# One output store for two batches: the shared 64-row blocks stored by a single transfer over 128 partitions

## Chip, cores and metric

The kernel runs on one core of one Trainium2 chip. The metric is device time in microseconds (us) of one execution. Where a profile is read, it is one profiled execution, and its span leaves out a little that the timed figure includes (435.0 us of span against 436.74 us for that same execution of the kernel before).

## The reference, cut to what matters

A causal attention with forget gates over 8 batches, 8 heads and 576 positions gives `x` of shape (8, 576, 512). A spectral mix over the sequence, with 64 modes, gives `y`, and the output is formed from both:

```python
u = x + y
return (u + np.maximum(u @ w_ch, 0.0)).astype(np.float32)   # (8, 576, 512)
```

Only the last stage matters here: the output, 9.44 MB in float32, is written to DRAM.

## The kernel before

A batch has 576 rows: four blocks of 128 and one of 64. To fill all 128 partitions, the 64-row blocks of two batches share one block: batch `b` lies on partitions 0 to 63, batch `b + 1` on 64 to 127. The last stage handles, for each of four pairs of batches, four "full" jobs (256 rows each) and then one shared block:

```python
jobs = []
for bp in range(B // 2):
    jobs += [(b, sb, 2) for b in (2 * bp, 2 * bp + 1) for sb in (0, 2)]
    jobs.append((2 * bp, 4, 1))          # the shared block
...
def emit_u(job, ps, split=False):
    uo = wpool.tile([128, 2, 2, D], F32, tag="wb", name="uo")   # ring of 9 buffers
    ...                                                         # ACT: uo[:, 0] <- PSUM

def emit_o(job, ps, uo, split=False):
    ...
        nc.vector.scalar_tensor_tensor(          # relu(u @ w_ch) + u
            uo[:, 1, bs, :], ps[1][:, bs, :], 0.0, uo[:, 0, bs, :],
            ALU.max, ALU.add,
        )
        if sb == 4:                              # shared block: two stores of 128 KB
            for h in range(2):
                eng = (nc.sync, nc.scalar)[h]
                eng.dma_start(
                    out[b + h, 512:576, :],
                    uo[64 * h : 64 * h + 64, 1, 0, :],
                )
        else:                                    # full job: 512 KB on SP
            nc.sync.dma_start(
                out[b, 128 * sb : 128 * sb + 256, :].rearrange(
                    "(p r) e -> p r e", r=2
                )[:, bs, :],
                uo[:, 1, bs, :],
            )
```

`nc.sync` issues on SP, `nc.scalar` on ACT. The first full job is stored in two halves, so there are 17 full-job stores, of which 5 come before the first shared block and 12 after it.

The softmax here doesn't subtract the row's maximum and nothing guards it: scores larger than these inputs give would overflow.

## Time and profile before

| | before |
|---|---|
| time, median of 3 runs | 439.09 us (435.85 to 439.66) |
| profiled span | 435.0 us |
| first output store issued | 404.62 us |
| last output store issued, landed | 430.33 us, 433.49 us |

The last three come from the trace's instruction records. The profile page of the kernel before shows the packets of all DMA traffic and of the hardware queues (q1 is SP's, q10 is ACT's; the columns are packets, MB, and the time that the packets took as a share of 16 engines' span):

```profile
span 435.0 us, 12214 instructions
...
DMA packets 50693, 97.37 MB, mean 224 GB/s; under 512 B 3760, under 2 KB 12944, under 8 KB 50640
...
q1 hardware_dynamic: 3632, 9.91, 6.3%
...
q10 hardware_dynamic: 320, 0.52, 0.3%
```

Packets under 512 B are completion packets of 4 bytes, apart from a few: on the hardware queues a transfer ends with one on each DMA engine that took part. The ACT queue carries only the four second halves of shared blocks: 320 packets = 4 x (64 rows + 16 completions). So each of those stores ran on 16 engines. This reading is used throughout: completion packets on a hardware queue count the engines.

The windows view of the kernel before, over the store stage (the last two columns are the mean busy share of the 16 DMA engines and the rate):

```profile
core 0: us, PE busy (x) PEld busy (x) DVE busy (x) ACT busy (x) POOL busy (x), PEclk, DMA share, GB/s
...
410.00:415.00 5.00, 4.90 (x63) 2.70 (x57) 3.69 (x5) 3.54 (x4) 0.26 (x1) 1.00 0.99 361
415.00:420.00 5.00, 4.55 (x59) 2.45 (x53) 4.11 (x4) 3.03 (x5) 0.00 (x0) 1.00 0.98 364
420.00:425.00 5.00, 4.40 (x52) 2.73 (x54) 4.02 (x5) 3.43 (x5) 0.00 (x0) 1.00 0.99 394
425.00:430.00 5.00, 3.50 (x40) 1.62 (x35) 4.33 (x5) 2.70 (x4) 0.00 (x0) 1.00 0.94 354
430.00:435.00 5.00, 0.00 (x0) 0.00 (x0) 0.29 (x1) 0.00 (x0) 0.00 (x0) 0.73 0.53 184
```

From 410 us on the DMA engines have next to no free time, 0.94 to 0.99, while PE, DVE and ACT each have some.

The view of the two store lines in the kernel before, L988 for shared blocks and L993 for full jobs (issue time on the queue in ns as least/median/most, and time from issue to landing):

```profile
L988 SPq DMA_DIRECT2D out_dram<-uo x4: 472/484/529, 410.1 to 430.3; - x4
L988 ACTq DMA_DIRECT2D out_dram<-uo x4: 501/504/570, 410.1 to 430.3; - x4
...
DMA to landing us min/median/max: 2.9/3.9/5.2
```

```profile
L993 SPq DMA_DIRECT2D out_dram<-uo x17: 332/333/367, 404.6 to 429.7; - x17
...
DMA to landing us min/median/max: 2.1/3.8/5.2
```

And what SP waited for in the kernel before (total us, times, longest); L1081 is the end of the program:

```profile
SPq L993 <- DVE uo L981: 20.0, 16, 4.0
...
SPq L1081 <- DMA out_dram<-uo: 2.6, 2, 1.7
```

### The profile page before, as it was taken

The numbers are of one execution on the slowest core, as the hardware profiler recorded it, in microseconds if no ns is written. First come the engines' busy times: TensorE is split into PE (matmuls) and PEld (weight loads), VectorE is DVE, ScalarE is ACT, GpSimd is POOL, SyncE is SP. The second block draws the span as 40 slices with busy tenths as digits, with TensorE's granted clock in tenths as the row PEclk, the third lists the DMA queues.
The fourth block names the chain that finished last, engine by engine and source line by source line (L and its number), as shares of the span: only waits on it lengthen the run. The fifth ranks groups of instructions, "written<-read, shape, count | busy, mean of one in ns | idle before, by whom it ended". The sixth has DMA issues, their size and how long they took to land.

```text
span 435.0 us, 12214 instructions
## 1 busy us (share of the span) xinstructions
PE 359.7 (83%) x5247; PEld 246.9 (57%) x5265; DVE 263.3 (61%) x658; ACT 225.3 (52%) x340; POOL 128.8 (30%) x202
## 2 busy tenths in 40 slices
PE   2687799999987877778878797899999987798984
PEld 1454566776665665565656565666665544554552
DVE  5677778877465655646657577523324544644875
ACT  3689378775626356364374554143344433633763
POOL 7333332153233233232333222232322232200600
PEclk9998689998868668577587779599999989989998
DMA  8999999999999999999999999999999999995697
GB/s 182 234 236 240 235 236 239 235 204 238 233 216 237 220 228 237 211 237 228 217 237 211 211 211 212 211 211 211 211 212 211 211 211 211 211 211 115 231 380 282
DMA packets 50693, 97.37 MB, mean 224 GB/s; under 512 B 3760, under 2 KB 12944, under 8 KB 50640
## 3 DMA queue, kind: packets, MB, share of 16 engines
q0 software_dynamic: 46688, 86.16, 101.2%
q1 hardware_dynamic: 3632, 9.91, 6.3%
q8 instruction: 41, 0.67, 0.6%
q10 hardware_dynamic: 320, 0.52, 0.3%
q14 instruction: 12, 0.10, 0.1%
HBM read 163.73 MB, written 9.44 MB: 398 GB/s over the span
## 4 chain that ended last, share of the span: by engine, by line
PE 35%; DMA 27%; ACT 12%; DVE 10%; issue 4%; DVEq 0%; POOL 0%; ACTq 0%
DMA wb<-in_moe_w_i_dram 26%; ACT E L559 8%; PE pav L597 7%; PE A L186 6%; PE ps L552 6%; PE tp L500 5%; PE px L640 3%; PE pz L806 2%; DVE QTs L515 2%; ACT KT L513 2%; PE vp L524 2%; DVE uo L981 2%; DVE XT L654 1%; DVE E L574 1%; PE pu L806 1%
## 5 line engine op out<-in xcount | busy, mean ns | idle before, releaser
L559 ACT ACTIVATE E<-ps 128x1024 bf16<-128x1024 f32 (+1 forms) x128 | 101.5, 854 | 24.1 <-PE ps L552 14.8
L186 PE MATMUL A<-XT,wb 128*128 128x16 bf16 x1984 | 70.1, 181 | 12.8 <-DMA wb<-in_moe_w_i_dram 7.8
L91 POOL DMA_DIRECT2D wb<-in_moe_w_r_dram x64 | 42.5, 663 | 126.6 <-PE A L186 30.2
L186 PEld LDWEIGHTS <-wb 128*128 128x128 bf16 x1984 | 63.4, 99 | 26.8 <-issue 11.6
L552 PE MATMUL ps<-QTs,KT 64*128 64x64 bf16 (+4 forms) x384 | 56.0, 315 | 18.1 <-ACT E L559 16.7
L91 POOL DMA_DIRECT2D wb<-in_moe_w_i_dram x64 | 42.4, 663 | 80.5 <-DMA wb<-in_moe_w_i_dram 38.1
L597 PE MATMUL pav<-va,E 128*128 128x65 bf16 (+1 forms) x1088 | 53.5, 206 | 4.2 <-DVE x_all L619 3.7
L597 PEld LDWEIGHTS <-E 128*128 128x128 bf16 (+1 forms) x1088 | 44.0, 112 | 20.1 <-issue 9.5
L574 DVE TENSOR_TENSOR E<-E,trimask 128x256 bf16<-128x256 bf16 (+2 forms) x128 | 37.3, 303 | 20.0 <-ACT E L559 19.7
L517 ACT COPY VT<-tp 128x640 bf16<-128x640 bf16 (+1 forms) x32 | 23.2, 755 | 33.2 <-PE tp L500 33.0
L845 ACT CAST XW<-pxw 128x512 bf16<-128x512 f32 x36 | 20.7, 587 | 35.7 <-PE pxw L838 30.8
L888 ACT CAST XW<-pB 128x512 bf16<-128x512 f32 x36 | 21.0, 586 | 31.8 <-PE pB L806 25.3
L552 PEld LDWEIGHTS <-KT 64*128 64x128 bf16 x384 | 19.0, 97 | 30.3 <-issue 21.3
L887 DVE CAST x_all<-pA 128x512 bf16<-128x512 f32 x36 | 24.9, 692 | 16.6 <-PE pA L806 15.7
L838 PE MATMUL pxw<-wch,yy 128*128 128x512 bf16 x133 | 33.7, 385 | 1.1 <-issue 0.5
L513 ACT COPY KT<-tp 128x640 bf16<-128x640 bf16 (+1 forms) x32 | 22.1, 754 | 22.2 <-PE tp L500 22.2
L515 DVE COPY QTs<-tp 128x640 bf16<-128x640 bf16 (+1 forms) x32 | 23.2, 768 | 14.2 <-PE tp L500 14.0
L619 DVE TENSOR_TENSOR x_all<-pav,rcp 128x384 bf16<-128x384 f32 x64 | 29.1, 455 | 0.8
L608 DVE RECIPROCAL rcp<-pav 128x6 f32<-128x6 f32 x64 | 12.1, 190 | 22.8 <-PE pav L597 22.1
L151 DVE TENSOR_TENSOR YTe<-A,Yacc 128x128 bf16<-128x128 f32 x16 | 5.9, 367 | 33.1 <-PE A L186 33.1
L806 PEld LDWEIGHTS <-ident_bf 64*64 64x64 bf16 (+1 forms) x300 | 15.9, 109 | 15.8 <-issue 8.2
L981 DVE SCALAR_TENSOR_TENSOR uo<-pz,uo 128x1024 f32<-128x1024 f32 (+1 forms) x21 | 21.9, 1070 | 4.6 <-PE pu L806 1.5
(141 smaller groups left out, 636.1 us busy)
## 6 DMA issues: line engine op xcount, KB each, us to landing
wb<-in_moe_w_r_dram POOLq DMA_DIRECT2D x62, 512.0 KB, 17.1
wb<-in_moe_w_i_dram POOLq DMA_DIRECT2D x62, 512.0 KB, 17.6
out_dram<-uo SPq DMA_DIRECT2D x15, 512.0 KB, 3.8
stv<-in_v_dram POOLq DMA_DIRECT2D x10, 576.0 KB, 15.4
stk<-in_k_dram POOLq DMA_DIRECT2D x11, 288.0 KB, 15.5
stq<-in_q_dram POOLq DMA_DIRECT2D x11, 288.0 KB, 15.3
wx<-in_v_dram POOLq DMA_DIRECT2D x5, 576.0 KB, 15.1
wx<-in_k_dram POOLq DMA_DIRECT2D x5, 288.0 KB, 15.7
```

The lines of the kernel that those rows point to most:

```text
L91: tc.keep_in_program_order(nc.gpsimd.dma_start(dst, src))
L186: nc.tensor.matmul(A[:, eb, mi, :], lhsT=w_of(mi, eb * 128), rhs=x_of(m), start=(i == 0), stop=(i == len(terms) - 1),)
L513: nc.scalar.copy(rows(KTs[pr % 2][:, :, 0:S]), tv)
L515: nc.vector.tensor_copy(rows(QT[pr][:, :, :]), tv)
L552: nc.tensor.matmul(ps[:, b, o : o + n], lhsT=KTs[pr % 2][bs, h, jb * 128 : (jb + 1) * 128], rhs=QT[pr][bs, h, jb * 128 + c0 : jb * 128 + c ...
L559: nc.scalar.activation(E[:, :, piece * 512 : piece * 512 + w], ps[:, :, 0:w], ACT.Exp, scale=scale,)
L574: nc.vector.tensor_tensor(dg, dg, tr, ALU.mult)
L597: nc.tensor.matmul(pav[64 * half : 64 * half + w, slot, :], lhsT=E[:, b, c : c + (w - 1) * st + 1 : st], rhs=va[:, jb, b, :], start=(n == ...
L619: nc.vector.tensor_tensor(xo, pi, ri, ALU.mult)
L806: return nc.tensor.matmul(p, lhsT=lhsT, rhs=rhs, start=first, stop=not first, skip_group_check=True)
L838: nc.tensor.matmul(pxw[:, :], lhsT=xT[:, eb, i * 128 : (i + 1) * 128], rhs=wch[:, eb, :], start=(eb == 0), stop=(eb == NDC - 1),)
L981: nc.vector.scalar_tensor_tensor(uo[:, 1, bs, :], ps[1][:, bs, :], 0.0, uo[:, 0, bs, :], ALU.max, ALU.add,)
```

## The change

The intent is to save one of two issues per shared block and to free ACT from storing. The destination is written as two batches x 64 rows x 512, the source is all 128 partitions:

```diff
                 if sb == 4:
-                    for h in range(2):
-                        eng = (nc.sync, nc.scalar)[h]
-                        eng.dma_start(
-                            out[b + h, 512:576, :],
-                            uo[64 * h : 64 * h + 64, 1, 0, :],
-                        )
+                    dst = out[b, 512:576, :]
+                    nc.sync.dma_start(
+                        bass.AP(
+                            tensor=dst.tensor,
+                            offset=dst.offset,
+                            ap=[[S * D, 2], [D, S - 512], [1, D]],
+                        ),
+                        uo[:, 1, 0, :],
+                    )
```

Bytes, addresses and the 2 KB contiguous runs are the same. The order of work on PE, DVE and POOL is unchanged.

## The prediction

> **What bounds the kernel now.** The change touches only the store stage, the last 30 us of a 435.0 us span (page). By the windows view the DMA engines are 0.98 to 0.99 busy at 361 to 394 GB/s from 410 to 425 us, all of it output stores. In the trace's packets a 4096-byte packet takes 163 ns and a 2048-byte one 84 to 94 ns, so each of the 16 engines gives about 25 GB/s: the stage is near its DMA limit. The last two stores are issued at 430.3 us and land at 433.5 us; 1.5 us of closing follow.
>
> **What the change does.** Four times, two 64-partition stores of 128 KB (SP 0.48 us, ACT 0.50 us of issue) become one 256 KB SP store. ACT loses four issues, 2 us in all; it is busy about 65% of this stage and its copies wait for PE, so that is worth tenths of a us. SP's issue count and the order on PE, DVE and POOL stay. Bytes and the 2 KB runs stay.
>
> **The hidden cost: how many engines share a store.** The old destination is 64 rows; the new one is 2 x 64 x 512, slowest dimension 2, beside 128 source partitions. The Trainium skill, "DMA: Bandwidth & Descriptors", section "Why a DMA increments its semaphore by 16 and not by 1", says a DMA uses the largest number of engines up to 16 that divides the slowest non-unit dimension of both sides. For the old stores that gives 16, and the trace agrees: sixteen 4-byte completion packets per store (320 packets on the ACT queue = 4 x (64 + 16)). For the new store it gives 2; no run here shows that yet.
>
> Then two engines move 64 packets of 2 KB each: 64 x 84 ns = 5.4 us per block instead of 0.7 us for both halves. They also carry their 8 packets (1.3 us) of every full store, queued behind. Per batch pair they need 4 x 1.3 + 5.4 = 10.6 us, while a pair now takes 6.76 us (418.62 to 425.38). So they fall behind from the first such store at 410 us: 14 full stores x 1.3 + 4 x 5.4 = 39.8 us, plus about 2 us of start and landing, puts the last landing near 450 to 452 us instead of 433.5. All of it is on the critical path, as only the end follows. Output buffers come round nine jobs later, so compute stalls little.
>
> **Prediction.** +17 us on 439 us (range +9 to +22): 456 us, 448 to 461. Chances: faster 0.01, same 0.12, slower 0.87.
>
> **What would show each step.** Packets under 512 B fall from 3760 to 3640 (128 completion packets removed, 8 added); with 16 engines kept, 3696. The ACT hardware queue (320 packets) vanishes; SP's has 3832. Issue to landing of the block stores grows from 3.9 us to about 7, 11, 15 and 19 us; the full stores behind them grow to some 7, 11, 14 us. After about 434 us no compute engine is busy and the windows show DMA near 0.12 (2 of 16), 50 GB/s, for 15 us. The chain ends with a long DMA out_dram<-uo piece.
>
> **What would make it wrong.** If the transfer is reshaped onto 16 engines, the time stays within 1 us. If engines run faster when only two are active, the loss shrinks toward 10 us; if waiting buffers or a full descriptor queue make SP issue the last block store late, it grows past 20 us.

## The result, and the profile after

| | before | after |
|---|---|---|
| time, median of 4 runs | 438.51 us (435.85 to 439.66) | 453.12 us (452.42 to 454.02) |
| ratio to before | | 1.0343 (1.0291 to 1.0395) |
| profiled span | 435.0 us | 451.3 us |
| first to last output store issued | 404.62 to 430.33 us | 404.58 to 434.52 us |
| from the first store's issue to the end of the span ("the store stage" below) | 30.4 us | 46.7 us |

A ratio here is the mean time of one kernel's fast runs over the mean of the other's fast runs of the same rounds, with a 95% interval, so it is not quite the ratio of the medians. (The kernel before had a fourth run in these rounds, so its median differs from that of the first table.) The first store is issued at the same time in both profiles; all 16.3 us of the longer span come after it.

The page of the kernel after:

```profile
span 451.3 us, 12194 instructions
...
DMA packets 50574, 97.37 MB, mean 216 GB/s; under 512 B 3641, under 2 KB 12825, under 8 KB 50521
...
q1 hardware_dynamic: 3832, 10.44, 6.7%
```

The ACT queue is gone. On SP the packets are 3632 + 200 = 3832: 4 x 64 data packets that ACT had, less 4 x 16 completions of the old SP halves, plus 4 x 2 completions of the new stores. Those 2 are the finding: **each merged store ran on two engines.** (Under 512 B there are 3641; one of them lies on an instruction queue, q14, that has 13 packets in this span and 12 before, and is not the stores'.)

The windows of the kernel after, over the store stage and beyond:

```profile
core 0: us, PE busy (x) PEld busy (x) DVE busy (x) ACT busy (x) POOL busy (x), PEclk, DMA share, GB/s
...
410.00:415.00 5.00, 4.90 (x63) 2.67 (x54) 3.67 (x4) 3.61 (x4) 0.23 (x1) 1.00 0.84 279
415.00:420.00 5.00, 4.54 (x59) 2.41 (x52) 4.11 (x4) 3.03 (x5) 0.00 (x0) 1.00 0.93 334
420.00:425.00 5.00, 4.39 (x52) 2.57 (x54) 4.00 (x5) 3.44 (x5) 0.00 (x0) 1.00 0.58 193
425.00:430.00 5.00, 3.42 (x40) 1.60 (x35) 2.75 (x3) 1.60 (x3) 0.00 (x0) 1.00 0.79 279
430.00:435.00 5.00, 0.00 (x0) 0.00 (x0) 1.82 (x2) 1.11 (x2) 0.00 (x0) 0.69 0.70 254
435.00:440.00 5.00, 0.00 (x0) 0.00 (x0) 0.00 (x0) 0.00 (x0) 0.00 (x0) 0.50 0.66 218
440.00:445.00 5.00, 0.00 (x0) 0.00 (x0) 0.00 (x0) 0.00 (x0) 0.00 (x0) 0.50 0.13 50
445.00:450.00 5.00, 0.00 (x0) 0.00 (x0) 0.00 (x0) 0.00 (x0) 0.00 (x0) 0.50 0.11 45
```

Before 435 us the engines' share already has holes (0.58 at 420 to 425), though the two engines with the merged stores are full. From 440 us no compute engine works and the share is 0.13 and 0.11, about 2 of 16, at 50 and 45 GB/s: two engines empty their queues. In the packets, the merged blocks run from 412.3 us (the first 2048-byte one) to 449.8 us (the last one), at 84 ns each when undisturbed; the late 4096-byte packets take 159 ns. In these 37.5 us each of the two engines has 12 x 8 packets of 4096 bytes and 4 x 64 of 2048 to move, 12 x 1.27 + 4 x 5.4 = 36.8 us of work: they hardly rest.

The store lines of the kernel after are L987 (shared blocks) and L996 (full jobs):

```profile
L987 SPq DMA_DIRECT2D out_dram<-uo x4: 522/598/1153, 410.0 to 434.5; - x4
```

```profile
L996 SPq DMA_DIRECT2D out_dram<-uo x17: 332/807/4821, 404.6 to 433.1; - x17
...
DMA to landing us min/median/max: 2.1/8.1/14.3
```

The full stores land after a median of 8.1 us in place of 3.8, up to 14.3 us, as far as the view can tell (it has the landing of 9 of the 17). Their issue on SP, at most 0.37 us before, takes up to 4.8 us. The view gives no landing for L987, since it expects 16 completions.

What SP waited for in the kernel after (L1084 is the end of the program):

```profile
SPq L996 <- DVE uo L981: 16.7, 14, 3.0
SPq L1084 <- DMA out_dram<-uo: 14.7, 6, 5.6
```

The final wait for stores grew from 2.6 to 14.7 us.

### The profile page after: what moved, and what is told of

It reads as the page before. It is cut to its first block, busy times and chain, and to the rows that moved or that the text cites. A ratio compares the mean times of both kernels' runs of the same rounds, so it can differ in the third digit from the quotient of the medians.

```text
span 451.3 us, 12194 instructions
## 1 busy us (share of the span) xinstructions
PE 365.6 (81%) x5247; PEld 251.2 (56%) x5265; DVE 263.4 (58%) x658; ACT 225.3 (50%) x340; POOL 128.9 (29%) x202
## 2 busy tenths in 40 slices
DMA packets 50574, 97.37 MB, mean 216 GB/s; under 512 B 3641, under 2 KB 12825, under 8 KB 50521
## 3 DMA queue, kind: packets, MB, share of 16 engines
q1 hardware_dynamic: 3832, 10.44, 6.7%
## 4 chain that ended last, share of the span: by engine, by line
PE 33%; DMA 27%; ACT 12%; DVE 9%; issue 4%; DVEq 0%; SPq 0%; POOL 0%; ACTq 0%
DMA wb<-in_moe_w_i_dram 25%; ACT E L559 8%; PE pav L597 7%; PE ps L552 6%; PE A L186 6%; PE tp L500 5%; DMA out_dram<-uo 3%; PE px L640 2%; PE vp L524 2%; ACT KT L513 2%; DVE QTs L515 2%; ACT VT L517 1%; DVE XT L654 1%; PE pz L806 1%; DVE E L574 1%
## 5 line engine op out<-in xcount | busy, mean ns | idle before, releaser
L186 PE MATMUL A<-XT,wb 128*128 128x16 bf16 x1984 | 70.2, 182 | 11.5 <-DMA wb<-in_moe_w_i_dram 6.7
L186 PEld LDWEIGHTS <-wb 128*128 128x128 bf16 x1984 | 63.6, 99 | 25.5 <-issue 11.9
L552 PE MATMUL ps<-QTs,KT 64*128 64x64 bf16 (+4 forms) x384 | 58.1, 327 | 14.4 <-ACT E L559 13.1
L597 PE MATMUL pav<-va,E 128*128 128x65 bf16 (+1 forms) x1088 | 56.3, 212 | 4.4 <-DVE x_all L619 3.6
L597 PEld LDWEIGHTS <-E 128*128 128x128 bf16 (+1 forms) x1088 | 46.6, 117 | 17.5 <-issue 7.1
## 6 DMA issues: line engine op xcount, KB each, us to landing
wb<-in_moe_w_r_dram POOLq DMA_DIRECT2D x62, 512.0 KB, 16.5
```

Of the source, the lines that this page charges most:

```text
L186: nc.tensor.matmul(A[:, eb, mi, :], lhsT=w_of(mi, eb * 128), rhs=x_of(m), start=(i == 0), stop=(i == len(terms) - 1),)
L552: nc.tensor.matmul(ps[:, b, o : o + n], lhsT=KTs[pr % 2][bs, h, jb * 128 : (jb + 1) * 128], rhs=QT[pr][bs, h, jb * 128 + c0 : jb * 128 + c ...
L597: nc.tensor.matmul(pav[64 * half : 64 * half + w, slot, :], lhsT=E[:, b, c : c + (w - 1) * st + 1 : st], rhs=va[:, jb, b, :], start=(n == ...
```

## The experiments

The theory: the number of DMA engines that share a store follows from the slowest dimension of its pattern, and the two engines that carry the merged blocks become the longest queue. Rivals are named in the expectations: (A) merging on one queue, (B) one transfer over two far regions, (C) SP being held at issue, (D) a fixed penalty for few engines or permuted rows, (E) only the tail of the last store; and, after some sizes had missed, (F) permuted rows, (G) the two queues disturbing each other, and (H) a backlog that is never caught up.

Each ran beside the kernel before on the same chip: the first four experiments share a chip and runs of before, as do the second four and the third four, on two other chips. "Difference" is of the medians, in us.

| run | engines per shared store | time | before | difference | ratio (95%) |
|---|---|---|---|---|---|
| the change | 2 | 453.12 | 438.51 | +14.6 | 1.0343 (1.0291 to 1.0395) |
| merged16 | 16 | 437.08 | 437.07 | 0.0 | 0.9999 (0.9972 to 1.0026) |
| two_on_sp | 16 | 437.49 | 437.07 | +0.4 | 1.0007 (0.998 to 1.0034) |
| perm_2 | 2 | 454.07 | 437.07 | +17.0 | 1.0391 (1.036 to 1.0422) |
| on_act | 2 | 453.15 | 437.07 | +16.1 | 1.0368 (1.0342 to 1.0394) |
| perm_4 | 4 | 446.39 | 437.76 | +8.6 | 1.0207 (1.0172 to 1.0242) |
| perm_8 | 8 | 440.88 | 437.76 | +3.1 | 1.0085 (1.005 to 1.0121) |
| last_only | 2, last block only | 442.42 | 437.76 | +4.7 | 1.0124 (1.0089 to 1.016) |
| first_three | 2, first three blocks | 449.22 | 437.76 | +11.5 | 1.0272 (1.0232 to 1.0312) |
| perm_16 | 16 | 436.77 | 437.61 | -0.8 | 0.9972 (0.9933 to 1.001) |
| sp_8 | 8 | 440.38 | 437.61 | +2.8 | 1.006 (1.0016 to 1.0104) |
| sp_4 | 4 | 449.54 | 437.61 | +11.9 | 1.0251 (1.0201 to 1.0301) |
| on_pool | made in software | 448.67 | 437.61 | +11.1 | 1.0242 (1.0198 to 1.0286) |

Merged16 and the runs named perm and sp with a number put rows of the shared block in the wrong places: a correct mapping of the same partitions cannot be written with those leading dimensions. Their addresses as a set, bytes and runs are those of the kernel.

### merged16: merged, but 16 engines

```diff
-                            ap=[[S * D, 2], [D, S - 512], [1, D]],
+                            ap=[[D, S - 512], [S * D, 2], [1, D]],
```

> One SP store of all 128 partitions per shared block, as in the change, but its destination is written as 64 x 2 x 512 instead of 2 x 64 x 512: same addresses, same 2 KB runs, same 256 KB, one issue. The rows of the block land permuted, so the result is wrong on purpose. Theory (the engine count follows from the slowest dimension): 16 completion packets per block store, packets under 512 B near 3696, SP queue 3888 packets, time within 1% of before, about 438.5 us. Rival A (merging on one queue, or losing the second queue, costs the time): as slow as the change, about 453 us. Rival B (one transfer that writes two regions of DRAM far apart is slow): also about 453 us.

The page of merged16:

```profile
span 435.5 us, 12194 instructions
...
DMA packets 50629, 97.37 MB, mean 224 GB/s; under 512 B 3696, under 2 KB 12880, under 8 KB 50576
...
q1 hardware_dynamic: 3888, 10.44, 6.3%
```

3696 small packets and 3888 on SP, as expected: 16 completions per store. The time is that of before to within 0.3%. One store, one queue, one issue and the same two far regions of DRAM cost nothing, so rivals A and B fall, and the change's intended saving is worth nothing either.

### two_on_sp: the second queue taken away, nothing merged

```diff
-                        eng = (nc.sync, nc.scalar)[h]
-                        eng.dma_start(
+                        nc.sync.dma_start(
```

> Two 64-partition stores per block as before, but both issued on SP. Theory: 16 engines each, time within 1% of before (438 to 440 us). Rival A (SP issuing alone, without the ACT queue beside it, costs the time): 445 us or more.

437.49 us, the same within 0.4%. Issuing all on SP costs nothing. The Trainium skill says so too ("DMA: Bandwidth & Descriptors", section "Issuing engines are not separate DMA queues"): several issuers share the same 16 engines and save only issue time, here 0.5 us a block that was hidden.

### perm_2: nothing merged, but two engines

Each 64-row store keeps its queue and gets a destination whose slowest dimension is 2 (even rows, then odd rows):

```diff
+                        dst = out[b + h, 512:576, :]
                         eng.dma_start(
-                            out[b + h, 512:576, :],
+                            bass.AP(
+                                tensor=dst.tensor,
+                                offset=dst.offset,
+                                ap=[[D, 2], [2 * D, 64 // 2], [1, D]],
+                            ),
                             uo[64 * h : 64 * h + 64, 1, 0, :],
```

> Two stores per block on SP and ACT as before, each 64 partitions, but each destination is written as 2 x 32 x 512 (even rows, then odd rows), so rows land permuted and the result is wrong on purpose. Nothing is merged. Theory: [...]the two carry 64 packets of 2 KB per block as in the change: about 453 us (450 to 455), DMA share near 0.12 in the last 8 us. Rivals A and B (merging, one queue, far regions): about 438.5 us.

The page of perm_2:

```profile
span 453.7 us, 12214 instructions
...
DMA packets 50581, 97.37 MB, mean 215 GB/s; under 512 B 3648, under 2 KB 12832, under 8 KB 50528
...
q1 hardware_dynamic: 3576, 9.91, 6.2%
...
q10 hardware_dynamic: 264, 0.52, 0.3%
```

264 packets on the ACT queue are 4 x (64 + 2), where before had 4 x (64 + 16). The windows of perm_2 near the end show the same signature as the change:

```profile
440.00:445.00 5.00, 0.00 (x0) 0.00 (x0) 0.00 (x0) 0.00 (x0) 0.00 (x0) 0.50 0.13 50
445.00:450.00 5.00, 0.00 (x0) 0.00 (x0) 0.00 (x0) 0.00 (x0) 0.00 (x0) 0.50 0.13 51
```

The loss is there, +17.0 us, without any merging. Together with merged16 this is the main result: the loss goes with the engine count, and not with the number of transfers or queues. That both stores' engines are the same two is what the 0.13 (2 of 16, not 4 of 16) shows.

### on_act: the merged store on the other queue

```diff
-                    nc.sync.dma_start(
+                    nc.scalar.dma_start(
```

> The changed store (2 x 64 x 512) issued on ACT instead of SP. Theory: the same two engines carry the same packets whatever queue feeds them, so about 453 us (450 to 455), though SP's long issues of up to 4.8 us should shrink to some 0.3 to 0.6 us. Rival C (the time is lost because SP is held up at issue behind the block store, so that the full stores start late): the full stores start on time and the end comes much earlier, 445 us or less.

The full stores (L996) of on_act, issue time on SP:

```profile
L996 SPq DMA_DIRECT2D out_dram<-uo x17: 332/333/972, 405.2 to 440.2; - x17
```

SP is hardly held any more (at most 0.97 us in place of 4.82), and the time does not move: 453.15 us. Its last windows end in the same thin tail of 2 engines in 16 (0.13), after a last full store that was issued only at 440.2 us:

```profile
440.00:445.00 5.00, 0.00 (x0) 0.00 (x0) 0.77 (x2) 0.00 (x0) 0.00 (x0) 0.50 0.45 175
445.00:450.00 5.00, 0.00 (x0) 0.00 (x0) 0.00 (x0) 0.00 (x0) 0.00 (x0) 0.50 0.13 47
```

This run alone does not refute rival C: its full stores still started late, though for another reason. By the view of L987 of on_act, ACT's copies waited 10.7 us for output buffers that the merged stores still held. What refutes it is the packets. If late starts had set the end, the two engines would have run out of work; but their 36.8 us of work filled 37.5 us in the change and 37.7 us in on_act (412.9 to 450.7 us). So late starts can have cost less than 1 us, and the long issues on SP are an effect of the queue, not the cause of the loss.

### perm_4 and perm_8: a dose of the engine count

As perm_2, with `ap=[[D, 4], [4 * D, 16], [1, D]]` and `ap=[[D, 8], [8 * D, 8], [1, D]]`.

> Two stores per block on SP and ACT, each destination written as 4 x 16 x 512 (rows land permuted, wrong on purpose). Theory: 4 engines per store, so four engines carry 32 packets of 2 KB per block, 2.7 us, beside 4 x 1.3 us of full stores: 7.8 us per batch pair against 6.76 us of production, so a small backlog: last landing near 439 us instead of 433.5, time +5.5 us on before (about 442.5, 440.5 to 444.5). Rival D (an engine count below 16 carries a fixed penalty, or the permuted rows do): as slow as with 2 engines, +16 us.

> As the run with 4 engines, but 8 x 8 x 512 (rows permuted, wrong on purpose). Theory: 8 engines, 16 packets per block, 1.35 us, so 6.55 us per batch pair, just below production: no backlog, only the last block is longer by 0.7 us: +0 to +1.5 us on before. Rival D: +16 us.

The packets of perm_4, and then of perm_8:

```profile
DMA packets 50598, 97.37 MB, mean 219 GB/s; under 512 B 3665, under 2 KB 12849, under 8 KB 50545
```

```profile
DMA packets 50630, 97.37 MB, mean 221 GB/s; under 512 B 3697, under 2 KB 12881, under 8 KB 50577
```

The counts are those for 4 and 8 engines: 3760 less 8 x 12 is 3664, less 8 x 8 is 3696, each with the one instruction-queue packet more. Rival D (a fixed penalty) falls, since the loss falls from +17.0 to +8.6 to +3.1. But both sizes missed: I expected +5.5 and at most +1.5. The next runs look for the reason.

### last_only and first_three: which blocks cost

The merged store under `if b == B - 2` (or `if b < B - 2`), the old pair of stores otherwise.

> Only the last of the four blocks is stored by the merged transfer, the other three as before. Theory: no backlog before it, so it costs its own 5.4 us less 0.7 us: +4.7 us on before (+3.5 to +5.5). Rival E (all the loss is the tail of the last transfer): +16 us.

> The first three blocks are stored by the merged transfer, the last as before. Theory: the two engines are backlogged from the first block on, so the last small stores wait in their queue: 12 x 1.27 + 3 x 5.4 + 0.7 us from 412.3 us gives a last landing near 444.8, +11 us on before (+9.5 to +12.5). Rival E (all the loss is the tail of the last transfer): 0 us.

The last block alone costs +4.7 us, as its own lengthening (64 x 84 ns less 8 x 84 ns = 4.7 us) says; the first three cost +11.5 us though the last store is spread over 16 engines. Rival E falls. The windows of last_only show a full stage and then a short thin tail, not a long one:

```profile
425.00:430.00 5.00, 3.86 (x44) 1.83 (x39) 4.33 (x5) 3.07 (x4) 0.00 (x0) 1.00 0.97 358
430.00:435.00 5.00, 0.00 (x0) 0.00 (x0) 0.67 (x2) 0.00 (x0) 0.00 (x0) 0.61 0.48 177
435.00:440.00 5.00, 0.00 (x0) 0.00 (x0) 0.00 (x0) 0.00 (x0) 0.00 (x0) 0.50 0.10 39
```

### perm_16, sp_8, sp_4: why the sizes of 4 and 8 missed

perm_16 is perm_2 with `ap=[[D, 16], [16 * D, 4], [1, D]]`. sp_8 and sp_4 are perm_8 and perm_4 with both stores on SP (`eng = nc.sync`).

> Two stores per block on SP and ACT, each destination written as 16 x 4 x 512 (rows permuted like the runs with 2, 4 and 8 engines, wrong on purpose), but 16 engines. A control: the runs with 4 and 8 engines lost 3 us more than expected (8.6 for 5.5, 3.1 for at most 1.5). Rival F (the permuted rows in DRAM cost by themselves): +2 to +3 us on before. Theory: within 1 us of before.

> As the run with 8 engines (8 x 8 x 512, rows permuted, wrong on purpose), but both stores issued on SP. Rival G (with few engines the two queues get in each other's way): at most +1.5 us on before. Rival H (the two queues have no part; the engines enter the first block already backlogged, and an extra 0.67 us per block for engines with no spare time is never caught up: 4 x 0.67 = 2.7 us): +2.5 to +4 us, as on two queues (+3.1).

> As the run with 4 engines (4 x 16 x 512, rows permuted, wrong on purpose), but both stores issued on SP. Rival G: about +5.5 us on before. Rival H: 4 x (2.7 - 0.67) = +8 us, as on two queues (+8.6).

The packets of perm_16:

```profile
DMA packets 50693, 97.37 MB, mean 223 GB/s; under 512 B 3760, under 2 KB 12944, under 8 KB 50640
```

With 16 engines (3760 small packets, as before) the permuted rows cost nothing: rival F falls. sp_8 lost +2.8 us, as H said, so the two queues are not needed for the extra loss and rival G falls. H's sum for each count, 4 x (packets per engine x 84 ns - 0.67 us), is set beside the measurement:

| engines | packets per engine and block | H's estimate | measured differences |
|---|---|---|---|
| 8 | 16 | 2.7 us | +3.1, +2.8 |
| 4 | 32 | 8.1 us | +8.6, +11.9 |
| 2 | 64 | 18.8 us | +14.6, +17.0, +16.1 |

H fits 8 engines and the lower of the two runs with 4. It does not fit everything: with 2 engines it is 2 to 4 us too high, with sp_4 about 4 us too low. sp_4 was also the least steady run (446.66 to 450.31 us).

Two things in the records narrow these misfits. First, part of sp_4's loss is not of the stores: its profiled execution issued the first store at 408.0 us, where the other profiles have 404.5 to 406.1. The store stage alone, from the first issue to the end of the span, takes in the profiles (one execution each):

| engines | runs | store stage, us | above before's 30.4 |
|---|---|---|---|
| 16 | merged16, two_on_sp, perm_16 | 30.0, 30.8, 30.3 | -0.4, +0.4, -0.1 |
| 8 | perm_8, sp_8 | 34.3, 33.2 | +3.9, +2.8 |
| 4 | perm_4, sp_4 | 38.2, 40.6 | +7.8, +10.2 |
| 2 | the change, perm_2, on_act | 46.7, 48.4, 46.7 | +16.3, +18.0, +16.3 |

So sp_4 exceeds H's 8.1 us by 2 and not by 4. Second, with 2 engines: from the first packet of a shared block to the last packet, an engine of the kernel before had 12 x 1.27 + 4 x 0.67 = 18.0 us of undisturbed packet time and took 21.0 us. These 3.0 us are rest, and packets that took longer than 159 or 84 ns. H's sum assumes that they stay, but with 2 engines 36.8 us took 37.5. The growth of 16.5 us is H's 18.8 less the 2.3 us of slack that were used up.

In the packets of perm_8 one more thing is seen: from 436.7 to 438.5 us only one packet is ever under way, so a single engine ended 1.8 us after all others, after 4096-byte packets that took 284, 534 and 694 ns. Why that engine was slow is not settled.

### on_pool: descriptors made in software

```diff
-                    nc.sync.dma_start(
+                    nc.gpsimd.dma_start(
```

> The changed store (2 x 64 x 512) issued on POOL, whose descriptors are made in software. Correct result. If these transfers too run on two engines, but on a next pair each time, the backlog does not add up on one pair, and the loss is about that of the last block alone: +4 to +7 us on before. If always on the same two engines: +14 to +18 us. If on 16 engines: within 2 us of before.

The page of on_pool (q0 is the software queue):

```profile
DMA packets 52165, 97.38 MB, mean 217 GB/s; under 512 B 5488, under 2 KB 14672, under 8 KB 52112
...
q0 software_dynamic: 48800, 87.22, 99.1%
```

+11.1 us lies between the two expected ranges, so the question asked is not answered. The transfer itself is another: the software queue has 2112 packets more, 528 per store. By size they are 64 of 4096 bytes, 16 completions and 448 of 8 bytes. From 441 to 445 us, 6 to 12 of the 4096-byte packets start in each us, which is what one or two engines do at 159 ns. The run shows only that the software path does not rescue this shape.

## Why the prediction was right

- **The engine count.** Predicted: 2 of 16 engines, from the Trainium skill's rule ("DMA: Bandwidth & Descriptors", section "Why a DMA increments its semaphore by 16 and not by 1") that a store uses the largest count up to 16 that divides the slowest dimension on both sides. Shown: 3832 packets on SP as predicted, and 16, 8, 4 or 2 completions in the other shapes, which the trace counts one by one. The trace agrees with the page in every hardware-queue case run here.
- **The cost.** Predicted: 64 packets x 84 ns = 5.4 us on each of two engines per block, all on the path. Shown: last_only costs the +4.7 us of one block, and the last landings were seen near 450 us (predicted 450 to 452). The measured 453.12 us lies in the range; the difference of +14.6 us is a little under the +17 predicted.
- **A count that was wrong, and did not show.** The text counted 14 full stores behind the first merged block. There are 12, so its sum was 2.6 us too long, which its wide range (+9 to +22) covered. Its "about 2 us of start and landing" is nearly used up by the start alone: the first merged packet runs at 412.3 us and not at 410. From there 12 x 1.27 + 4 x 5.4 = 36.8 us gives 449.1 us, and the trace has 449.8.
- **The step that was too simple.** "Per batch pair they need ... 10.6 us, while a pair now takes 6.76 us" treats 6.76 us as room that an engine has for its stores. For two engines this made no difference, but my expectations for 4 and 8 engines came from the same comparison and were 2 to 3 us low. The DMA share of 0.98 to 0.99 in the windows of before had said that there was little room; and the stores of before landed after 5.2 us at most, early in the stage, and 2.9 us at its end, so the stage starts with a backlog and only drains it slowly.
- **The small packets of the profile.** 3641 for 3640, the ACT queue gone, DMA share 0.13 and 50 GB/s at 440 to 445 us: as predicted. The thin tail lasts about 11 us, not 15, since the other 14 engines had late full stores to finish until 438 us: SP was held at issue, which the prediction had only as a possibility.
- **What was not seen as predicted.** The landing of the merged stores cannot be read from the view. The full stores behind them landed after 8.0, 12.0 and 14.3 us where 7, 11 and 14 were named. The wait at the end is in SP's waits (14.7 us) and not at the end of the chain of waits, which ends on DVE. The last store was issued at 434.5 and not at 430.3 us: SP was held at issue, and ACT waited 2.9 us for output buffers. That did not set the end: on_act has its last issue later still, at 440.8 us, and the same time, and in both runs the two engines had work almost all the time (36.8 of 37.5 and of 37.7 us).
- **Still open.** Why sp_4's store stage is 2.4 us longer than perm_4's, and why its first store came 2.4 us later; why one engine was slow in perm_8; which engines the software path used.

## What to carry to other kernels

Before merging two stores, look at the slowest dimension of both sides of the merged pattern (the runs here varied the destination's) and not only at bytes and contiguous runs: a leading dimension of 2 put a store on 2 of 16 DMA engines and cost 3.4% of the whole kernel, where a leading dimension of 64 cost nothing. Count completion packets of the hardware queues in the profile to see how many engines a transfer really used. In this stage, already full of DMA traffic, an issue saved was worth nothing, and engine time added to a few engines was hardly hidden at all.

## What the Trainium skill lacked or had wrong

- "DMA: Bandwidth & Descriptors", section "Why a DMA increments its semaphore by 16 and not by 1": the rule of the engine count held for 2, 4, 8 and 16 engines. It gives no measured cost for a low count; here 2 engines for four 256 KB stores cost +14.6 us, and 8 engines still +3.
- The same page, section "Bandwidth", advises batching into larger transfers and does not say there that a batched shape can lose engines; the warning stands only further down, in its table "Rules for kernel authors": an outermost dimension below 16 confines a transfer to at most that many engines. The warning can outweigh the advice: with one 256 KB store on 2 engines per block the kernel was slower than with two of 128 KB on 16 (453.12 against 438.51 us).
- On none of the pages: how long an issue takes while the engines that it feeds are behind. SP's issue of a full store rose from 0.33 us to as much as 4.82 us when SP also issued the merged stores, and to 0.97 us at most when ACT did.
- On none of the pages: the software path moved this store with 448 extra packets of 8 bytes per store. That all 16 engines post a completion there, as "DMA: Bandwidth & Descriptors", section "Why a DMA increments its semaphore by 16 and not by 1", says, agrees with 528 = 64 + 16 + 448; so completions are no count of the engines there.
